# Idle products, tiles loaded singly, stores on another queue and sums loaded first in a fused S4 convolution and feed-forward kernel

## The chip, the cores and the metric

One Trainium2 chip, one core. The metric is device time in microseconds (us) of one execution. In the text P is 128, the number of partitions; PE is TensorE, DVE VectorE, ACT ScalarE, POOL GpSimd and SP SyncE. A DMA is issued from the queue of an engine (`nc.sync`, `nc.scalar`, `nc.gpsimd`), and the issuing instruction takes its turn among that engine's other instructions.

## What is computed

The input x has 2048 rows of 576. The result is x plus two branches of its layer norm, all in float32:

```python
xn  = (x - mean) / sqrt(var + 1e-5)                  # over the 576 columns
# S4: a kernel K of length 2048 per column, 128 complex states
A, B, C = A_re + 1j*A_im, B_re + 1j*B_im, C_re + 1j*C_im
dt  = exp(log_dt)
K   = einsum("dn,dnl,dn->dl", C, exp(dt*A*l), dt*B).real
y   = irfft(rfft(pad(xn.T)) * rfft(pad(K)))[:, :2048].T + xn * Dskip
h   = silu(xn @ w1)                                  # w1: 576 x 4608
out = x + y + h @ w2                                 # w2: 4608 x 576
```

## The kernel before

**The feed-forward part.** The rows stand in 16 tiles of 128 (`j` from 0 to 15), four tiles in a block of 512; tiles 0 to 7 are the first half, 8 to 15 the second. The 36 pieces of 128 hidden features are taken in chunks of four (`c`; `FT` is 4, `NCH` 9). For float32 accuracy each operand is split in a high and a low part (`h`, `l`): ScalarE copies the high part in the rounded type, VectorE subtracts it from the source, and three products replace one. `load_w1` fetches two pieces of w1 (tile `w1r`), `split_w1` makes `w1h` and `w1l` of it; `load_w2` and `split_w2` do the same for w2 (`w2r`, `w2`). `up` (L281) makes the hidden features of a block in `ph`, takes the SiLU and splits it in `gh` and `gl`; `down` (L301) multiplies them with w2 in `po`, for two halves of 288 columns, and VectorE adds `po` to `acc`, which holds x at first. After the last chunk of the first half, `down` stores `acc[j]` to `dr0` in DRAM and, for each odd j, loads two tiles of the second half in the buffers that came free (L326 to L328).

**Layer norm and transposes.** `phase0` (L200) takes a pair of tiles: `load_x` (L162) loads x in four quarters of 32 partitions, `norm` takes the statistics on VectorE, the power -0.5 on GpSimd, and makes `xn` on VectorE for even tiles and on ScalarE for odd ones. `normed` transposes `xn` on TensorE (`put_xt`, tile `pt`) and splits it in `xh`, `xl`, `x4`. For the blocks of the second half the transposed tile goes to one buffer `xt` and from there to `dxt` in DRAM; `next_xt` loads it again later. `xn` is stored to `dxn` for the convolution.

**The convolution** goes on beside that as a generator `side()` (L1022), in stages: `kgen` makes K with sines and exponentials, `spread` reads `xn` from `dxn` and makes the first transform (stores to `d1u` on GpSimd's queue, L158, from one buffer `u1`), `spectral` multiplies in the frequency domain and stores to `d2` (from tile `yo`), and `tail` (L947) adds the result. For the second half's tiles `conv` adds inside `down`, in the same bank as the products. For tiles 0 to 7 `last(j)` adds to `r0`, the sums of the first half loaded from `dr0`: `add_conv` makes 16 small products in `py` from `ys`, VectorE adds `py` to `r0`, and every second `last` stores two tiles of `r0` to the output on GpSimd's queue. There are two `r0` buffers of two tiles each and six `ys` buffers (`AHEAD`).

**The second half** of the feed-forward part runs in a form with fewer products (`wino_ffn`, L427): products in `pa`, `pb`, `pc` (L444, L450) with weights that VectorE first combines, and sums of them on VectorE, `f` (L519) among them.

**The order.** `weave(fg, 276, sd)` interleaves the two generators: each time `ffn()` has yielded, `side()` goes on as long as its own mark, a share of 276 steps, lies behind. `tail()` yields such marks for its steps: the loads from `tail_at[0]` on, `tail_at[1]` apart, and the `last(j)` from `tail_at[2]` on, `tail_at[3]` apart. Before it, `side()` and `ffn()` are advanced once or twice by hand:

```python
    sd = side()
    next(sd)
    fg = ffn()
    next(fg)
    next(sd)
    weave(fg, 276, sd)
```

What is issued in that order is placed by a scheduler, which simulates the engines and builds the order of each engine from it; `tc.high_priority()` lifts an instruction and `behind(ins)` keeps what follows behind another instruction. `pins` keeps the instructions that serve for that. One change in the program so shifts the built order of every engine in many places.

Of the kernel before, what the change touches and what calls it, by code (L numbers as in the profile page):

```python
# [10 lines left out]
F32 = mybir.dt.float32  # L11
# [30 lines left out]
def kernel(  # L42
# [30 lines left out]
    def quarters(v, engines):  # L73

        for q in range(4):
            yield slice(32 * q, 32 * q + 32), v[q // 2, q % 2], engines[q % len(engines)]
# [85 lines left out]
    def load_x(j, pool, tag, engines):  # L162

        t = pool.tile([P, 2, D], F32, tag=tag, name=f"{tag}{j}")
        for ps, v, eng in quarters(xv, engines):
            eng.dma_start(t[ps], v[:, j:j + 2])
        pairs[j] = t
        return t[:, 0, :], t[:, 1, :]

# [5 lines left out]
    def norm(p0, js, xs):  # L175

        n = len(js)
        st = p0.tile([P, 2, 2, 6], F32, tag="st", name="st")
        mv = p0.tile([P, 2, 2], F32, tag="mv", name="mv")
        for i in range(n):  # L180
            for h in range(2):
                nc.vector.bn_stats(out=st[:, i, h, :], in_=xs[i][:, h * HD:(h + 1) * HD])
            nc.vector.bn_aggr(out=mv[:, i, :], in_=st[:, i, :, :])
        sd = p0.tile([P, 2], F32, tag="sd", name="sd")
        mb = p0.tile([P, 2], F32, tag="mb", name="mb")
        nc.vector.tensor_scalar(sd[:, :n], mv[:, :n, 1], 1e-5, None, op0=ALU.add)
        pins["sd"] = nc.gpsimd.tensor_tensor(sd[:, :n], sd[:, :n], mhalf[:, :n], op=ALU.pow).ins
        xn = p0.tile([P, 2, D], F32, tag="xn", name="xn") if js[0] < 8 else pairs[js[0]]
        for i, j in enumerate(js):
            if j % 2 == 0:  # L190
                pins["xn"] = nc.vector.tensor_scalar(xn[:, i, :], xs[i], mv[:, i, 0:1], sd[:, i:i + 1],
                                                 op0=ALU.subtract, op1=ALU.mult).ins
            else:
                nc.vector.scalar_tensor_tensor(mb[:, i:i + 1], mv[:, i, 0:1], -1.0, sd[:, i:i + 1],
                                               op0=ALU.mult, op1=ALU.mult)
                nc.scalar.activation(xn[:, i, :], xs[i], AF.Identity,
                                     scale=sd[:, i:i + 1], bias=mb[:, i:i + 1])
        return xn

    def phase0(p0, js):  # L200
        j0 = js[0]
        if j0 < 8:
            xs = load_x(j0, accp, "acc", (nc.sync, nc.scalar) if j0 < 4 else (nc.sync,))
            acc.update(zip(js, xs))
        else:
            xs = load_x(j0, p0, "xj", (nc.sync,))
        if j0:
            normed(p0, js, xs)
        else:
            for j, xj in zip(js, xs):  # L210
                normed(p0, (j,), (xj,))

    def normed(p0, js, xs):
        xn = norm(p0, js, xs)
        for i, j in enumerate(js):
            b, jj = divmod(j, 4)
            if b < 2:
                if jj == 0:
                    xts[b] = new_xt(b)
                c = slice(jj * P, (jj + 1) * P)  # L220
                xh, xl, x4 = xts[b]
                put_xt(xh[:, :, c], xl[:, :, c], x4[:, c], xn[:, i, :])
            else:
                xt = p0.tile([P, 9, P], F32R, tag="xt", name="xt", bufs=1)
                put_xt(xt[:, 0:4, :], xt[:, 4:8, :], xt[:, 8, :], xn[:, i, :])
                nc.sync.dma_start(dxt[b - 2][:, :, jj * P:(jj + 1) * P], xt.bitcast(F32))
        nc.sync.dma_start(dxn[:, js[0]:js[0] + len(js)], xn[:, :len(js)])

    def ffn():
        w2v = w2.rearrange("(t p) d -> p t d", p=P)  # L230
# [31 lines left out]
        def load_w2(half, c, t):  # L262

            first = half == 0 and c == 0
            r2 = (pa if first else kfp).tile([P, D], F32, tag="w2r", name="w2r", bufs=4 if first else 2)
            pins["load"] = nc.sync.dma_start(r2, w2v[:, c * FT + t, :]).ins
            R2[half, c, t] = r2
# [33 lines left out]
        def down(blk, jj, terms=None):  # L301
            half, c, b = blk
            j = 8 * half + 4 * b + jj
            js = slice(jj * P, (jj + 1) * P)
            if half == 1 and c == NCH - 1 and jj % 2 == 0:
                for i, (pool, tag) in enumerate(((ps2, "ps2"), (ps1, "ps1"))):
                    begun[j + i] = [pool.tile([P, 512], F32, tag=tag, name="po") for _ in range(2)]
                conv((j, j + 1), (begun[j], begun[j + 1]))
                for i in range(2):
                    conv_load(j + i + AHEAD)  # L310
            terms = terms or [(G[blk, t], W2[half, c, t]) for t in range(FT)]
            for h in range(2):
                hs = slice(h * HD, (h + 1) * HD)
                po = begun[j][h] if j in begun else ps2.tile([P, 512], F32, tag="ps2", name="po")
                n = 0
                for gs, ws in terms:
                    for g, w in ((0, 0), (0, 1), (1, 0)):
                        pins["pe"] = nc.tensor.matmul(po[:, :HD], gs[g][:, js], ws[:, w, hs],  # L318
                                                      start=n == 0 and j not in begun, stop=n == 3 * len(terms) - 1,
                                                      skip_group_check=j in begun).ins  # L320
                        n += 1
                with tc.high_priority():
                    nc.vector.tensor_add(acc[j][:, hs], po[:, :HD], acc[j][:, hs])  # L323
            if half == 0 and c == NCH - 1:
                rows = slice(j * P, (j + 1) * P)
                nc.sync.dma_start(dr0[rows, :], acc[j])  # L326
                if j % 2:
                    acc[7 + j], acc[8 + j] = load_x(7 + j, accp, "acc", (nc.sync,))  # L328

        def next_xt(b):  # L330
            xt = new_xt(2 + b)
# [4 lines left out]

        for t in (0, 2):
            load_w1(0, 0, t)
        for t in (0, 2):
            split_w1(0, 0, t)  # L340
        for t in range(FT):
            load_w2(0, 0, t)
        for t in range(FT):
            split_w2(0, 0, t)
        yield 0
# [601 lines left out]
    def tail():  # L947

        r0s = {}

        def load_r0(j):
            r0s[j] = yp.tile([P, 2, D], F32, tag="r0", name="r0", bufs=2)
            nc.sync.dma_start(r0s[j], dr0[j * P:(j + 2) * P, :].rearrange("(i p) d -> p i d", p=P))

        def last(j):
            add_conv(j, r0s[j - j % 2][:, j % 2, :])
            conv_load(j + AHEAD)
            if j % 2:
                store(r0s[j - 1], j - 1, (nc.gpsimd,))

        steps, at = [], tail_at[0]
        for j in range(8):
            for f in (conv_load, load_r0)[j >= AHEAD:2 - j % 2]:
                steps.append((at, f, j))
                at += tail_at[1]
        steps += [(tail_at[2] + j * tail_at[3], last, j) for j in range(8)]
        for at, f, j in sorted(steps, key=lambda v: v[0]):
            yield at
            with behind(pins["load"]):
                f(j)  # L970
# [51 lines left out]
    def side():  # L1022
        nonlocal s4, kl, yp, pa, kfp, tail_at
        marks = (0.1357, 0.613, 0.855)
        tail_at = (0.893, 0.003, 0.930, 0.005)
        with tc.tile_pool(name="pa", bufs=4) as pa:
            for js in ((0, 1), (2, 3), (4, 5), (6, 7)):
                with behind(pins["xt3"] if js[0] > 2 else None):
                    phase0(pa, js)
                pins[f"xt{js[1]}"], pins[f"xt{js[1]}s"] = pins["xt_v"], pins["xt_s"]  # L1030
                if js[0] == 2:
                    yield 0
            yield 0
        with tc.tile_pool(name="kf", bufs=1) as kfp:
            for n in ("f", "rho", "phi"):
                kf[n] = kfp.tile([P, D], F32, name=n + "T")
            with tc.tile_pool(name="nat", bufs=1) as nat, tc.tile_pool(name="pb", bufs=2) as pb:
                nt = natural(nat)
                tiles = iter(range(8, NJ, 2))
                for at, tables in ((0.0, 1), (0.02, 0), (0.035, 0), (gate_of(1), 1), (0.06, 0), (gate_of(2), 1), (0.08, 0), (0.085, 1)):  # L1040
                    yield at
                    if tables:
                        next(nt, None)
                    else:
                        j = next(tiles)
                        with behind(pins["gl"]):
                            phase0(pb, (j, j + 1))
            with behind(pins["sd"]):
                nc.gpsimd.dma_start(f1, cf1)
            nc.sync.dma_start(vt, cv)  # L1050
# [19 lines left out]
        yp = ctx.enter_context(tc.tile_pool(name="yp", bufs=3))  # L1070
        yield from tail()

    sd = side()
    next(sd)
    fg = ffn()
    next(fg)
    next(sd)
    weave(fg, 276, sd)
    for j in range(8, 14, 2):
        store(pairs[j], j, (nc.sync, nc.gpsimd))  # L1080
# [80 lines left out]
```

## Time and profile before

| | us |
|---|---|
| median of 3 timed runs | 1136.39 |
| lowest, highest | 1133.1, 1138.12 |
| the profiled execution | 1141.59 |
| its span in the trace | 1139.8 |
| busy: TensorE | 1104.0 (97%) |
| busy: VectorE | 955.5 (84%) |
| busy: ScalarE | 721.1 (63%) |
| busy: GpSimd | 113.4 (10%) |
| DMA | 176.04 MB, mean 154 GB/s |

The trace is of one execution. Its views: busy time by engine; the waits (who waited for whom, total us, times, longest); the chain of work that ended last, followed back from the end; the timeline of instructions; windows (the share of each engine in a stretch, with the granted clock of TensorE, 1.00 being full speed); and the DMA issues, with the size and the median time from issue to landing. A matmul's end is modelled with its pipeline, so the durations of two products overlap and a busy TensorE is not one at its peak.

### The profile page before, as it was taken

The numbers are of one execution on the slowest core, as the hardware profiler recorded it, in microseconds if no ns is written. First come the engines' busy times: TensorE is split into PE (matmuls) and PEld (weight loads), VectorE is DVE, ScalarE is ACT, GpSimd is POOL, SyncE is SP. The second block draws the span as 40 slices with busy tenths as digits, with TensorE's granted clock in tenths as the row PEclk, the third lists the DMA queues.
The fourth block names the chain that finished last, engine by engine and source line by source line (L and its number), as shares of the span: only waits on it lengthen the run. The fifth ranks groups of instructions, "written<-read, shape, count | busy, mean of one in ns | idle before, by whom it ended". The sixth has DMA issues, their size and how long they took to land.

```text
span 1139.8 us, 23099 instructions
## 1 busy us (share of the span) xinstructions
PE 1104.0 (97%) x9101; PEld 991.5 (87%) x9101; DVE 955.5 (84%) x1631; ACT 721.1 (63%) x1269; POOL 113.4 (10%) x206
## 2 busy tenths in 40 slices
PE   6999999999999999999989999999999999999798
PEld 5998989888988899899988889999989899998576
DVE  6698898999999999999979988988888888884432
ACT  4665456676677666676747646887867777772210
POOL 1001000000000000000000002112112112210111
PEclk9999999999999999999989999999999999999899
DMA  9456523536263625376844137556455556547964
GB/s 274 131 160 197 165 97 101 144 109 167 83 166 108 188 86 150 109 218 215 230 124 115 54 64 219 153 172 181 141 161 148 171 171 187 176 121 180 260 172 109
DMA packets 171405, 176.04 MB, mean 154 GB/s; under 512 B 88432, under 2 KB 136576, under 8 KB 170656
## 3 DMA queue, kind: packets, MB, share of 16 engines
q1 hardware_dynamic: 150128, 120.91, 38.4%
q0 software_dynamic: 20784, 52.76, 14.7%
q8 instruction: 72, 1.18, 0.4%
q10 hardware_dynamic: 384, 0.89, 0.3%
q14 instruction: 37, 0.30, 0.1%
HBM read 112.00 MB, written 62.60 MB: 153 GB/s over the span
## 4 chain that ended last, share of the span: by engine, by line
PE 52%; DVE 21%; DMA 10%; issue 7%; ACT 7%; SPq 1%; POOL 1%; DVEq 0%; ACTq 0%; POOLq 0%
PE po L318 23%; PE ph L289 12%; DMA w1r<-in_B_w_dram 5%; PE pb L444 3%; DVE acc L323 2%; PE kp L855 2%; PE pc L444 2%; DMA w2r<-in_B_w_dram 1%; DVE th L798 1%; DMA ys<-d 1%; DVE S L834 1%; DVE C L834 1%; PE pb L986 1%; PE pu L986 1%; DVE gl L299 1%
## 5 line engine op out<-in xcount | busy, mean ns | idle before, releaser
L318 PE MATMUL po<-w,gh 128*128 128x288 f32 x2304 | 479.5, 297 | 8.2 <-ACT gh L298 3.8
L318 PEld LDWEIGHTS po<-w,gh 128*128 128x128 f32 x2304 | 378.2, 189 | 26.7 <-issue 5.6
L318 PE MATMUL po<-w,gl 128*128 128x288 f32 x1152 | 337.3, 297 | 0.4 <-DVE gl L299 0.4
L318 PEld LDWEIGHTS po<-w,gl 128*128 128x128 f32 x1152 | 216.2, 189 | 3.9 <-issue 1.4
L323 DVE TENSOR_TENSOR acc<-po,acc 128x288 f32<-128x288 f32 x296 | 130.5, 451 | 61.9 <-PE po L318 60.6
L289 PE MATMUL ph<-xh,w1h 128*128 128x512 f32 (+1 forms) x368 | 99.7, 389 | 0.9 <-ACT xh L124 0.6
L289 PE MATMUL ph<-xl,w1h 128*128 128x512 f32 (+1 forms) x368 | 99.3, 387 | 0.0
L289 PE MATMUL ph<-xh,w1l 128*128 128x512 f32 (+1 forms) x368 | 98.1, 383 | 0.0
L297 ACT ACTIVATE gf<-ph 128x512 f32<-128x512 f32 (+1 forms) x92 | 53.1, 577 | 48.8 <-PE ph L291 36.0
L289 PEld LDWEIGHTS ph<-xl,w1h 128*128 128x128 f32 x368 | 67.7, 192 | 12.9
L289 PEld LDWEIGHTS ph<-xh,w1l 128*128 128x128 f32 x368 | 66.8, 190 | 12.0
L289 PEld LDWEIGHTS ph<-xh,w1h 128*128 128x128 f32 x368 | 65.5, 192 | 11.3 <-ACT xh L124 0.9
L814 ACT ACTIVATE c<-th,magic 128x1040 f32<-128x1040 f32 x36 | 42.0, 1168 | 39.8 <-DVE C L835 31.6
L158 POOL DMA_DIRECT2D d1u<-u x32 | 17.3, 542 | 460.2 <-ACT u L157 460.2
L299 DVE TENSOR_TENSOR gl<-gf,gh 128x512 fp32r<-128x512 f32 (+1 forms) x92 | 60.6, 660 | 2.9 <-ACT gh L298 2.7
L298 ACT CAST gh<-gf 128x512 fp32r<-128x512 f32 (+1 forms) x92 | 55.2, 601 | 10.2 <-PE po L318 9.0
L816 ACT ACTIVATE c<-th 128x1040 f32<-128x1040 f32 x36 | 38.7, 1074 | 31.1 <-DVE th L815 31.1
L361 ACT CAST w1h<-w1r 128x512 fp32r<-128x512 f32 (+2 forms) x56 | 34.5, 619 | 37.1 <-DMA w1r<-in_B_w_dram 36.0
L892 POOL DMA_DIRECT2D m<-in_cm_dram x64 | 34.5, 539 | 223.7 <-PE pu L986 140.3
L362 DVE TENSOR_TENSOR w1l<-w1r,w1h 128x512 fp32r<-128x512 f32 (+2 forms) x56 | 38.3, 685 | 21.7 <-ACT w1h L361 21.7
L834 DVE TENSOR_TENSOR S<-th,C 128x1024 f32<-128x1024 f32 x36 | 43.9, 1219 | 9.8 <-ACT th L817 9.7
L461 DVE TENSOR_TENSOR gl<-gf,gh 128x512 fp32r<-128x512 f32 x56 | 37.8, 687 | 10.8 <-ACT gh L460 10.5
(268 smaller groups left out, 2372.2 us busy)
## 6 DMA issues: line engine op xcount, KB each, us to landing
w1r<-in_B_w_dram SPq DMA_DIRECT2D x35, 512.0 KB, 4.2
dw<-w SPq DMA_DIRECT2D x28, 576.0 KB, 4.7
w<-dw POOLq DMA_DIRECT2D x28, 576.0 KB, 5.8
w2r<-in_B_w_dram SPq DMA_DIRECT2D x44, 288.0 KB, 5.0
d1u<-u POOLq DMA_DIRECT2D x32, 288.0 KB, 2.7
d1k<-stage SPq DMA_DIRECT2D x18, 512.0 KB, 7.0
ur<-d1u SPq DMA_DIRECT2D x32, 288.0 KB, 4.0
kr<-d1k SPq DMA_DIRECT2D x32, 288.0 KB, 3.0
```

The source lines that it names most:

```text
L289: nc.tensor.matmul(ph, w[:, kt, :], v[:, kt, a:e], start=n + kt == 0, stop=False)
L297: nc.scalar.activation(gf, ph, AF.Silu)
L298: pins["gh"] = nc.scalar.copy(gh, gf).ins
L299: pins["gl"] = nc.vector.tensor_sub(gl, gf, gh).ins
L318: pins["pe"] = nc.tensor.matmul(po[:, :HD], gs[g][:, js], ws[:, w, hs], start=n == 0 and j not in begun, stop=n == 3 * len(terms) - 1, ski ...
L323: nc.vector.tensor_add(acc[j][:, hs], po[:, :HD], acc[j][:, hs])
L362: nc.vector.tensor_sub(l[:, :k], src, h[:, :k])
L444: pins["pe"] = nc.tensor.matmul(dst, a[:, kt], v[:, kt], start=start and n == 0, stop=stop and n == 5, skip_group_check=True).ins
L461: pins["gl"] = nc.vector.tensor_sub(gl, gf, gh).ins
L814: nc.scalar.activation(c65, th, AF.Identity, bias=magic)
L816: nc.scalar.activation(c65, th, AF.Abs)
L834: nc.vector.tensor_mul(ov3, t[:, :, 0:64].rearrange("n d (x y) -> n d x y", y=32), mv3)
```

## The change

At the outset, 14 products of a zeroed tile with itself go to TensorE ahead of all else (their result is used by nobody). Tiles 0 and 1 are loaded one by one, each in four quarters from SyncE's and ScalarE's queues, where the pair was one set of four loads; tiles 2 and 3 are loaded from SyncE's queue alone, and behind the loads of the first weights: `phase0` now yields between the load and the rest, `ffn()` between its loads and splits, and the driver advances the two in turn. The first weights of w2 are loaded ahead of the splits of w1. Where one tile is normalised alone (tiles 0 and 1), `xn` is made on VectorE for the odd tile too, and the work on tiles 2 and 3 is kept behind the last VectorE step of tile 1.

The stores to `dxt`, `dxn` and `dr0`, and the loads of the second half's tiles in `acc`, go to GpSimd's queue, where they were in SyncE's.

In the tail, each `r0` load comes ahead of the `ys` load that it was behind, and the first `last` is marked at 0.936 for 0.930.

```diff
--- before.py
+++ after.py
@@ -162,8 +162,12 @@
     def load_x(j, pool, tag, engines):
 
         t = pool.tile([P, 2, D], F32, tag=tag, name=f"{tag}{j}")
-        for ps, v, eng in quarters(xv, engines):
-            eng.dma_start(t[ps], v[:, j:j + 2])
+        for i in range(j, j + 2, 1 if j == 0 else 2):
+            for ps, v, eng in quarters(xv, engines):
+                if j == 0:
+                    eng.dma_start(t[ps, i], v[:, i])
+                else:
+                    eng.dma_start(t[ps], v[:, j:j + 2])
         pairs[j] = t
         return t[:, 0, :], t[:, 1, :]
 
@@ -187,7 +191,7 @@
         pins["sd"] = nc.gpsimd.tensor_tensor(sd[:, :n], sd[:, :n], mhalf[:, :n], op=ALU.pow).ins
         xn = p0.tile([P, 2, D], F32, tag="xn", name="xn") if js[0] < 8 else pairs[js[0]]
         for i, j in enumerate(js):
-            if j % 2 == 0:
+            if j % 2 == 0 or n == 1:
                 pins["xn"] = nc.vector.tensor_scalar(xn[:, i, :], xs[i], mv[:, i, 0:1], sd[:, i:i + 1],
                                                  op0=ALU.subtract, op1=ALU.mult).ins
             else:
@@ -200,12 +204,14 @@
     def phase0(p0, js):
         j0 = js[0]
         if j0 < 8:
-            xs = load_x(j0, accp, "acc", (nc.sync, nc.scalar) if j0 < 4 else (nc.sync,))
+            xs = load_x(j0, accp, "acc", (nc.sync, nc.scalar) if j0 == 0 else (nc.sync,))
             acc.update(zip(js, xs))
+            yield
         else:
             xs = load_x(j0, p0, "xj", (nc.sync,))
         if j0:
-            normed(p0, js, xs)
+            with behind(pins["xt1"] if j0 == 2 else None):
+                normed(p0, js, xs)
         else:
             for j, xj in zip(js, xs):
                 normed(p0, (j,), (xj,))
@@ -223,8 +229,8 @@
             else:
                 xt = p0.tile([P, 9, P], F32R, tag="xt", name="xt", bufs=1)
                 put_xt(xt[:, 0:4, :], xt[:, 4:8, :], xt[:, 8, :], xn[:, i, :])
-                nc.sync.dma_start(dxt[b - 2][:, :, jj * P:(jj + 1) * P], xt.bitcast(F32))
-        nc.sync.dma_start(dxn[:, js[0]:js[0] + len(js)], xn[:, :len(js)])
+                nc.gpsimd.dma_start(dxt[b - 2][:, :, jj * P:(jj + 1) * P], xt.bitcast(F32))
+        nc.gpsimd.dma_start(dxn[:, js[0]:js[0] + len(js)], xn[:, :len(js)])
 
     def ffn():
         w2v = w2.rearrange("(t p) d -> p t d", p=P)
@@ -323,9 +329,9 @@
                     nc.vector.tensor_add(acc[j][:, hs], po[:, :HD], acc[j][:, hs])
             if half == 0 and c == NCH - 1:
                 rows = slice(j * P, (j + 1) * P)
-                nc.sync.dma_start(dr0[rows, :], acc[j])
+                nc.gpsimd.dma_start(dr0[rows, :], acc[j])
                 if j % 2:
-                    acc[7 + j], acc[8 + j] = load_x(7 + j, accp, "acc", (nc.sync,))
+                    acc[7 + j], acc[8 + j] = load_x(7 + j, accp, "acc", (nc.gpsimd,))
 
         def next_xt(b):
             xt = new_xt(2 + b)
@@ -336,10 +342,12 @@
 
         for t in (0, 2):
             load_w1(0, 0, t)
+        yield 0
+        for t in range(FT):
+            load_w2(0, 0, t)
+        yield 0
         for t in (0, 2):
             split_w1(0, 0, t)
-        for t in range(FT):
-            load_w2(0, 0, t)
         for t in range(FT):
             split_w2(0, 0, t)
         yield 0
@@ -960,7 +968,7 @@
 
         steps, at = [], tail_at[0]
         for j in range(8):
-            for f in (conv_load, load_r0)[j >= AHEAD:2 - j % 2]:
+            for f in (load_r0, conv_load)[j % 2:2 - (j >= AHEAD)]:
                 steps.append((at, f, j))
                 at += tail_at[1]
         steps += [(tail_at[2] + j * tail_at[3], last, j) for j in range(8)]
@@ -1022,12 +1030,21 @@
     def side():
         nonlocal s4, kl, yp, pa, kfp, tail_at
         marks = (0.1357, 0.613, 0.855)
-        tail_at = (0.893, 0.003, 0.930, 0.005)
+        tail_at = (0.893, 0.003, 0.936, 0.005)
         with tc.tile_pool(name="pa", bufs=4) as pa:
+            zero = pa.tile([P, P], F32, name="zero", bufs=1)
+            nc.vector.memset(zero, 0.0)
+            idle = pss.tile([P, 512], F32, tag="pss", name="idle")
+            for _ in range(14):
+                nc.tensor.matmul(idle[:, :P], zero, zero, start=True, stop=True)
             for js in ((0, 1), (2, 3), (4, 5), (6, 7)):
                 with behind(pins["xt3"] if js[0] > 2 else None):
-                    phase0(pa, js)
+                    for _ in phase0(pa, js):
+                        if js[0] == 2:
+                            yield 0
                 pins[f"xt{js[1]}"], pins[f"xt{js[1]}s"] = pins["xt_v"], pins["xt_s"]
+                if js[0] == 0:
+                    yield 0
                 if js[0] == 2:
                     yield 0
             yield 0
@@ -1044,7 +1061,8 @@
                     else:
                         j = next(tiles)
                         with behind(pins["gl"]):
-                            phase0(pb, (j, j + 1))
+                            for _ in phase0(pb, (j, j + 1)):
+                                pass
             with behind(pins["sd"]):
                 nc.gpsimd.dma_start(f1, cf1)
             nc.sync.dma_start(vt, cv)
@@ -1070,11 +1088,9 @@
         yp = ctx.enter_context(tc.tile_pool(name="yp", bufs=3))
         yield from tail()
 
-    sd = side()
-    next(sd)
-    fg = ffn()
-    next(fg)
-    next(sd)
+    sd, fg = side(), ffn()
+    for g in (sd, fg, sd, fg, sd, fg, sd):
+        next(g)
     weave(fg, 276, sd)
     for j in range(8, 14, 2):
         store(pairs[j], j, (nc.sync, nc.gpsimd))
```

## The prediction

> **What bounds the kernel now.** I read the busy shares first, then what TensorE waited for, then the granted clock around the long waits, then the chain of waits at each of those places. The span, the busy shares, and TensorE's rows of the waits (total us, times, longest us):
>
> ```profile
> span 1139.8 us, 23099 instructions
> ```
> ```profile
> PE 1104.0 (97%) x9101; PEld 991.5 (87%) x9101; DVE 955.5 (84%) x1631; ACT 721.1 (63%) x1269; POOL 113.4 (10%) x206
> ```
> ```profile
> PE pt L123 <- DVE xn L191: 8.9, 1, 8.9
> PE pb L450 <- DVE f L519: 8.1, 1, 8.1
> PE po L318 <- ACT gh L298: 3.8, 2, 3.3
> ...
> PE po L318 <- ACT w L275: 1.7, 1, 1.7
> ```
>
> TensorE is busy for 1104.0 of 1139.8 us, and the change takes no product of the computation away. So a microsecond saved on another engine is worth nothing unless it shortens one of TensorE's few waits: 8.9 us at the outset, 8.1 us near the end, 3.3 us at 577 us and 1.7 us at 95 us. A wait costs more than itself, since the clock falls with it. The windows around the three later waits (length, each engine's busy time, granted clock, DMA share, GB/s):
>
> ```profile
> 94.00:102.00 8.00, 6.10 (x28) 4.93 (x27) 7.29 (x15) 6.05 (x9) 0.00 (x0) 0.79 0.85 247
> 576.00:586.00 10.00, 6.72 (x32) 6.49 (x32) 6.89 (x10) 5.50 (x12) 0.31 (x1) 0.66 0.54 171
> 1058.00:1071.00 13.00, 4.89 (x34) 3.71 (x34) 4.65 (x11) 1.14 (x2) 0.00 (x0) 0.74 1.09 255
> ```
>
> The clock was 0.79, 0.66 and 0.74, that is 1.7, 3.4 and 3.4 us of full clock missing. Part of that falls inside the waits, so I count 1.7, 2.0 and 2.5 us of slow products on top (the cuts in the last two are my choice). The places cost 3.4, 5.3 and 10.6 us.
>
> **The outset.** The chain of waits there, three rows of the timeline, and the sizes of what is loaded:
>
> ```profile
> 3.27 7.66 DMA w1r<-in_B_w_dram
> ...
> 11.03 1.35 ACT w1h L257 x2
> 12.38 0.49 ACT xh L124
> ```
> ```profile
> 8.91 1.12 PE L123 MATMUL pt<-ident,xn 128*128 128x128 f32 x4 [8.91 <-DVE xn L191]
> ```
> ```profile
> 12.92 2.07 PE L289 MATMUL ph<-xh,w1h 128*128 128x256 f32 x8 [0.57 <-ACT xh L124]
> ```
> ```profile
> 21.89 0.64 PE L289 MATMUL ph<-xh,w1h 128*128 128x256 f32 x4
> ```
> ```profile
> acc<-in_A_u_dram SPq DMA_DIRECT2D x28, 144.0 KB, 3.6
> ```
> ```profile
> w1r<-in_B_w_dram POOLq DMA_DIRECT2D x1, 512.0 KB, 8.5
> ```
>
> The first real product starts at 12.92, not when tile 0 is normalised: the first weights land at 10.93, ScalarE splits them until 12.38 and only then copies tile 1's xh. Loading tile 0 singly can bring the transposes forward by some 2 us, but in the built order ScalarE still has both w1h casts ahead of tile 1's copy, so the start remains the landing plus 2.0. Ahead of that landing stood four tiles, eight quarters of 144 KB, and the first weight piece, of which 512 KB are in the row: 1664 KB. In the changed order two tiles and two pieces stand there, 1600 KB, and the later pair of tiles behind them. So the first piece lands at about the same time or somewhat earlier, and the second, which stood behind four tiles, with it. I let the start move by 0 to 1 us.
>
> The fourteen idle products are over by then. A 128x128 product took at most 0.28 us (1.12 over 4), so they cover 4 us at most, and TensorE then has only ten transposes until the weights are in, a gap of 2 us or more. A 128x256 product takes 0.26 us at 12.92 (2.07 over 8) and at most 0.16 at 21.89, so the slow stretch costs some 40% of its time, 2.5 us if it lasts 6. The row of 94 to 102 shows the clock missing 1.7 us around a wait of 1.7, so I expect it low again for a part of the first products. The Trainium skill, "TensorE: Matmul & The Clock Gate", Part 1, says the clock is released after about 3.4 us of sustained products and falls back after an idle window of that length; the 1.7 us that a wait of 1.7 cost at 95 us is shorter than that, and by that rule the warm-up would last through a gap of 2 to 3 us. If it does, VectorE is next: four statistics of tiles 2 and 3 now stand between its w1l splits, and the transposes of those tiles stand in TensorE's order ahead of the second halves. I take a gain of 1.5 us; the ends are a loss of 1 (tiles 2 and 3, loaded later, hold TensorE) and a gain of 5 (start 1 earlier, 2.5 from the full clock, 1.5 of holds between the early products).
>
> **The stores on gpsimd's queue.** At 95 us the chain, ScalarE's row there, and the transit of 576 KB on either queue:
>
> ```profile
> 79.09 8.09 DMA dxt<-xt
> ...
> 91.78 4.15 DMA w2r<-in_B_w_dram
> ```
> ```profile
> 87.26 0.59 ACT L124 CAST xt<-pt 128x512 fp32r<-128x512 f32 x1 [6.10 <-DMA dxt<-xt]
> ```
> ```profile
> dw<-w SPq DMA_DIRECT2D x28, 576.0 KB, 4.7
> w<-dw POOLq DMA_DIRECT2D x28, 576.0 KB, 5.8
> ```
>
> There is one xt buffer, so ScalarE sat 6.1 us until the store of the tile before had landed, 8.09 us after its issue, because it went into SyncE's queue behind tile loads and most of a weight load. Its casts then came late, the w2r buffer was freed late, the next w2r was asked for at 91.78, and TensorE stood. On gpsimd's queue nothing is ahead of the store. The nearest rows for 576 KB are 4.7 us (SyncE) and 5.8 us (gpsimd); I take 5.8, by the queue, so what stands behind it moves 2.3 us earlier and the 1.7 us wait goes: a gain of 3.4, bounds 0 and 3.4. What is late next is still ScalarE at the following store, held 2 us less. On gpsimd the powers of tiles 12 and 13 are now queued behind three such stores, but in the built order VectorE writes those xt ahead of using the powers, so they cannot hold VectorE longer than its own order does.
>
> At 577 us the w2r load stood on SyncE behind stores of acc and loads into it. The chain, SyncE's waits, and gpsimd's largest:
>
> ```profile
> 573.41 4.97 DMA w2r<-in_B_w_dram
> ```
> ```profile
> SPq L166 <- DMA dr<-acc: 13.7, 4, 4.4
> ...
> SPq L326 <- DVE acc L323: 11.5, 4, 4.8
> ```
> ```profile
> POOL d1u L158 <- ACT u L157: 460.2, 32, 46.3
> ```
>
> SyncE's 13.7 and 11.5 us of waiting go to gpsimd, which stands idle 460 us ahead of its d1u stores. The w2r loads then wait only for their buffer. I take 4 of the 5.3 us, since a buffer may hold a part; bounds 0 and 5.3. The cover is that slack: two d1u stores now stand directly behind loads of acc that wait for a store to dr0; what it costs if the slack is not there is the last rival.
>
> The Trainium skill, "SBUF — State Buffer", section "SBUF: two separate sides", speaks against all of this: a DMA issued from GpSimd's queue needs descriptors, which GpSimd cannot write while VectorE holds the port that they share. VectorE is 84% busy, yet the two rows for 576 KB differ by 1.1 us, and no run here shows more of it.
>
> **The tail.** SyncE's longest wait, the chain, the rate, the transits, and two rows that price TensorE's products:
>
> ```profile
> SPq L993 <- DMA d<-yo: 15.6, 1, 15.6
> ```
> ```profile
> 1031.28 2.36 DMA d<-yo
> ```
> ```profile
> 1055.07 10.61 DMA w1r<-in_B_w_dram
> ```
> ```profile
> 1066.79 0.69 DVE f L519
> ```
> ```profile
> 1040.00:1060.00 20.00, 18.85 (x150) 15.16 (x148) 6.08 (x13) 2.41 (x5) 1.96 (x4) 1.00 1.11 247
> ```
> ```profile
> r<-dr SPq DMA_DIRECT2D x4, 576.0 KB, 8.0
> out_dram<-r POOLq DMA_DIRECT2D x16, 144.0 KB, 6.0
> ```
> ```profile
> 1099.14 3.19 PE po L318 x24
> 1102.33 1.38 PE pb L444 x6
> ```
>
> SyncE idles 15.6 us because the first ys load needs the last yo in DRAM. Then twelve ys loads, two r0 loads and the last w1r go out at once, the DMA engines are full (share 1.11 at 247 GB/s), and w1r lands at 1065.7 (1055.07 + 10.61), 34.4 us after the last yo store was issued. VectorE has the split of that w1r ahead of f, which ends at 1067.5, so TensorE wanted f at 1059.4, 28.1 us after that store. With r0 of tiles 0 and 1 first in the queue, its 576 KB move inside the 15.6 us; at 247 GB/s that frees 2.4 us. Counting both built orders by the last two rows (0.133 and 0.23 us per product), TensorE has 30.2 us of products from the last yo to that point after the change and 27.8 before: 2.4 us more. So the wait shrinks from 8.1 to 3.3 us and the slow clock behind it from 2.5 to about 1.3: a gain of 6.0. Bounds: 2.4 (only the load counts) and 10.6.
>
> The later start of the added convolutions (0.936 for 0.930) has a price. By the same count tile 0's py products stand 61.5 us of products before the end, not 72.2, and tile 4's follow tile 1's by only 9.6 us instead of 13.3. In between, r0 must be stored (6.0 us) and the next one loaded into its buffer (8.0 us), with some 2 us to add and issue: 16 us. VectorE would wait up to 6.4 us there; TensorE's three po buffers and the products that don't need r0 cover some 4 to 5 by my estimate. I book 0, bounds 0 and 4, the far end with the slow clock behind the remaining 2.
>
> **The sum.** 1.5 + 3.4 + 4.0 + 6.0 = 14.9 us. The profiled execution took 1141.59 (span 1139.8), so it would take 1126.7. The median of the three timed runs, 1136.39, is 5.2 below that execution; against it the forecast is 1136.4 − 14.9 = 1121.5.
>
> **The rivals.**
> *The stores land no sooner on gpsimd*, by the rule above, or because the DMA engines are as full for one queue as for the other: the waits at 95 and 577 stay, 1121.5 + 3.4 + 4.0 = 1129. For: 5.8 is above 4.7. Against: 8.09 was a place in a queue, not a rate. Chance 0.17.
> *The r0 wait takes the place of the w1r wait*: of the tail's 6, 2.4 stay and 4 are lost, 1121.5 + 7.6 = 1129. For: 16 against 9.6 + 5 us. Against: with the backlog cleared earlier, the store and the load meet emptier engines than those of their rows. Chance 0.14.
> *The change does not do what it says*: both of these, or the same waits at other places, since the order that the scheduler builds differs in nearly all stages; 1136. Chance 0.10.
> *Slower: loads of acc hold the d1u stores on gpsimd.* There is one u1 buffer. A d1u store held by 4.4 us (the longest wait for dr<-acc) and some 2 us of issues holds ScalarE's next u1 copy, and in its order gh, on which TensorE waits. Two stores stand so: 12.8 us, and 2 us of slow clock behind each. With the gain at 577 lost as well: 1121.5 + 4 + 16.8 = 1142. It decides if ScalarE copies the next u1 within 6.4 us of the last. Against: the 460 us of idle over 32 stores, 14 us each. Chance 0.13.
>
> **How the numbers follow.** The forecast has 0.46. Its own range is 1111 (start 5, tail 10.6, 577 whole: 9.4 less) to 1132 (start −1, 577 nothing, tail 4 less: 10.5 more). With the two rivals at 1129 and the one at 1136, I give 1111 to 1138; the slow case is left out. About 0.5% (5.7 us) is what a measurement of this kernel can tell from no change. Below 1130.7 fall nearly all of the forecast and some 0.20 of the two at 1129: 0.64. Within 0.5% lie the rest of these and over half of the case at 1136: 0.19. Slower: 0.17.
>
> **What would show it.** Right: an r0 load stands ahead of SyncE's wait for d<-yo; f's wait at L450 falls to about 3 us; no wait for w at 95 or for gh at 577, and the clock full there; the first product at 12 to 13 us. Wrong: a wait of VectorE for r<-dr with TensorE behind it; dxt landing in 8 us or more from gpsimd; ScalarE waiting for d1u near 550. The forecast is wrong as a whole if TensorE's idle time does not shrink by some 10 us.

## The result and the profile after

The changed kernel is slower: 1152.83 us median (1149.97 to 1154.7) against 1136.38 (1133.1 to 1138.12), a ratio of 1.0146 with a 95% interval of 1.0113 to 1.0179. The profiled execution took 1154.7 us, its span is 1152.5. The page after, span and busy shares:

```profile
span 1152.5 us, 23170 instructions
...
PE 1112.4 (97%) x9129; PEld 997.0 (87%) x9129; DVE 958.5 (83%) x1632; ACT 718.9 (62%) x1268; POOL 136.6 (12%) x247
```

TensorE is as busy as before, in shares, over a span that is 12.7 us longer; GpSimd's share rose by 2 points. Its waits (total us, times, longest us):

```profile
PE ph L295 <- ACT w1h L263: 7.1, 2, 6.2
PE po L324 <- DVE acc L329: 5.5, 6, 1.8
PE pb L458 <- DVE f L527: 4.3, 1, 4.3
PE pu L994 <- ACT kb L920: 3.0, 1, 3.0
PE po L324 <- ACT gh L468: 2.8, 1, 2.8
PE pt L123 <- DVE xn L195: 2.6, 2, 2.3
```

The four waits that the prediction went after are gone or shorter: 8.9 at the outset is 2.6 beside the idle products, 8.1 for f is 4.3, those for gh at 577 and for w at 95 have left the list. In their place stand others: 6.2 us for w1h, 3.0 for kb and 2.8 for gh, none of which the kernel before had at these places. The windows around them (length, busy time of each engine, granted clock, DMA share, GB/s):

```profile
560.00:580.00 20.00, 13.76 (x74) 12.23 (x72) 12.92 (x20) 9.26 (x12) 3.91 (x8) 0.83 0.64 183
700.00:712.00 12.00, 9.24 (x43) 7.85 (x42) 5.83 (x13) 8.73 (x19) 1.28 (x3) 0.83 0.81 273
908.00:916.00 8.00, 4.96 (x32) 4.36 (x31) 3.65 (x8) 3.38 (x8) 0.00 (x0) 1.00 0.41 143
```

Where the 12.7 us lie is seen when both traces are cut at equal work, not at equal times. The windows of the kernel before, from the point at which TensorE has done 140 us of products to 480, 600 and 940, and those of the changed kernel between the same points:

```profile
162.00:545.00 383.00, 381.59 (x4016) 344.02 (x4015) 366.78 (x540) 262.19 (x391) 16.78 (x31) 1.00 0.48 141
545.00:686.00 141.00, 136.12 (x1307) 122.34 (x1307) 123.20 (x182) 82.25 (x125) 6.90 (x13) 0.98 0.43 110
686.00:1037.00 351.00, 347.50 (x2173) 320.54 (x2172) 294.44 (x567) 266.13 (x571) 62.55 (x116) 1.00 0.55 164
```
```profile
163.00:552.00 389.00, 384.01 (x4029) 344.26 (x4028) 375.35 (x552) 264.02 (x394) 20.99 (x39) 1.00 0.48 140
552.00:693.00 141.00, 134.69 (x1290) 120.69 (x1289) 122.73 (x181) 83.16 (x125) 16.10 (x30) 0.98 0.43 111
693.00:1053.00 360.00, 351.40 (x2174) 322.66 (x2173) 295.10 (x566) 265.53 (x571) 60.94 (x114) 0.99 0.54 162
```

The middle stretches take 875 us before and 890 after: 15 us, of which the tail gives some 2.5 back. In the last of them, 9 us longer, the change edits nothing but the place of the first r0 load in its last 10 us: no step of it touches the convolution's spectral stage and the products of the second half's form (`wino_ffn`) that run there. What differs in it is only the order that the scheduler built. TensorE's listed waits there add up to 8.4 us, for 3.4 before, and the granted clock was low for longer, behind the two long waits of the changed kernel and behind the one (2.0 us, for kb) of the kernel before:

```profile
707.00:715.00 8.00, 6.28 (x17) 5.10 (x18) 6.94 (x13) 7.46 (x16) 0.00 (x0) 0.57 0.33 87
916.00:920.00 4.00, 4.00 (x12) 3.08 (x12) 3.85 (x10) 2.76 (x6) 0.53 (x1) 0.57 0.24 52
```
```profile
834.00:839.00 5.00, 4.44 (x18) 3.96 (x19) 4.26 (x11) 4.58 (x11) 0.54 (x1) 0.66 0.21 36
```

That is some 5 us of full clock missing for 1.7. Waits and clock together so account for nearly all of the 9 us. In the first of the stretches TensorE was idle for 5.0 us, for 1.4 before, with the clock full: behind several short waits (2.1 us for additions to acc, 1.4 for kt). The rest of what that stretch lost lies in intervals too short to be listed, and its cause stays open. The chain of the changed kernel at the two long waits of the last stretch, and gpsimd's timeline at the first:

```profile
699.42 6.86 DMA kr<-d1k
...
706.35 0.67 ACT kh L985
...
707.05 1.11 ACT gf L467 x2
708.16 0.52 ACT gh L468
```
```profile
698.62 2.12 POOL L479 DMA_DIRECT2D w<-dw  x4 [6.14 <-PE po L324]
```
```profile
906.67 6.43 DMA w1r<-in_B_w_dram
...
913.20 0.51 ACT w1h L369
...
914.87 0.40 ACT kb L920
```

In both, ScalarE's order puts a copy that needs a load (kh, w1h) ahead of the one on which TensorE waits (gh, kb), and the load takes 6 to 7 us, about twice its median of 3.1 (kr) or 3.6 to 3.7 (the pieces of w1r); at the first place four loads of w were issued within the same 2 us. The kernel before has such loads too (one of kr, issued at 696 us, took 6.7 us to land), but TensorE has no wait at these places.

The theory from this: **the order**. The edits move the scheduler's simulated times, it builds another order for nearly all stages, and this order has more and longer waits; the edits' own costs are small. The rivals: **the queue** (the stores and loads on gpsimd's queue cost, above all at 560 us) and **the outset** (the idle products and the reordered loads cost).

### The profile page after: what moved, and what is told of

Its sections match the earlier page's. It is cut to its first block, busy times and chain, and to the rows that moved or that the text cites. A ratio compares the mean times of both kernels' runs of the same rounds, so it can differ in the third digit from the quotient of the medians.

```text
span 1152.5 us, 23170 instructions
## 1 busy us (share of the span) xinstructions
PE 1112.4 (97%) x9129; PEld 997.0 (87%) x9129; DVE 958.5 (83%) x1632; ACT 718.9 (62%) x1268; POOL 136.6 (12%) x247
## 4 chain that ended last, share of the span: by engine, by line
PE 61%; DVE 19%; DMA 8%; ACT 6%; issue 3%; SPq 1%; POOL 0%; DVEq 0%; ACTq 0%; POOLq 0%
PE po L324 28%; PE ph L295 12%; PE pb L452 4%; DMA w1r<-in_B_w_dram 3%; PE pc L452 2%; PE kp L863 2%; PE pb L994 2%; PE pu L994 1%; PE pk L994 1%; DVE acc L329 1%; DMA acc<-in_A_u_dram 1%; PE z L878 1%; DVE th L806 1%; DVE gl L305 1%; DVE th L823 1%
## 5 line engine op out<-in xcount | busy, mean ns | idle before, releaser
L324 PEld LDWEIGHTS po<-w,gh 128*128 128x128 f32 x2304 | 378.3, 189 | 29.8 <-DVE acc L329 9.2
L370 DVE TENSOR_TENSOR w1l<-w1r,w1h 128x512 fp32r<-128x512 f32 (+2 forms) x56 | 38.3, 684 | 19.1 <-ACT w1h L369 18.9
L842 DVE TENSOR_TENSOR S<-th,C 128x1024 f32<-128x1024 f32 x36 | 43.8, 1218 | 9.0 <-ACT th L825 9.0
L469 DVE TENSOR_TENSOR gl<-gf,gh 128x512 fp32r<-128x512 f32 x56 | 38.0, 686 | 10.7 <-ACT gh L468 10.4
```

What stands on the lines that cost most here:

```text
L370: nc.vector.tensor_sub(l[:, :k], src, h[:, :k])
L842: nc.vector.tensor_mul(ov3, t[:, :, 0:64].rearrange("n d (x y) -> n d x y", y=32), mv3)
```

## The experiments

Every ratio is to the kernel before, run beside it. First, each part by itself, where the built order could be held.

**Ten idle products.** The kernel before with

```diff
+            idle = pss.tile([P, 512], F32, tag="pss", name="idle")
+            for _ in range(10):
+                nc.tensor.matmul(idle[:, :P], zero, zero, start=True, stop=True)
```

> The kernel before with ten idle products at the outset and nothing else; the built order of every engine stays that of the kernel before beyond the first 40 us. Theory of the order (the loss of 16 us lies in the order that the scheduler builds, which differs in nearly all stages): as before, within 3 us, waits at 95, 577, 832 and 1059 us at their old places. Theory of the outset (the products themselves, with the clock that they set, cost time): slower by several us.

1138.62 us, ratio 1.0011 (0.9994 to 1.0028): no change that can be measured. The products themselves neither cost nor gain anything clear.

**Fourteen**, `range(14)`.

> The kernel before with fourteen idle products and nothing else. Four products more, some 1 us, shift the scheduler's simulated times so that the built order becomes another one from the first stages on; from about 600 us it is that of the changed kernel up to the tail. Theory of the order: 5 to 12 us slower than the ten products, with waits near 706 and 912 us as in the changed kernel and none at 832. Theory of the queue (the loss comes from the stores and loads on gpsimd's queue) and theory of the outset: within 1 us of the ten products.

1139.98, ratio 1.0028 (1.0009 to 1.0048). Waits of 1.6 and 1.9 us appear where the changed kernel has 2.8 and 3.0, so the order brings the waits; but it is only 1.4 us slower than the ten, not 5 to 12, since this kernel's stretch ahead of 680 us is better than that of before. An order is not good or bad as a whole.

**The tail alone:**

```diff
-            for f in (conv_load, load_r0)[j >= AHEAD:2 - j % 2]:
+            for f in (load_r0, conv_load)[j % 2:2 - (j >= AHEAD)]:
-        tail_at = (0.893, 0.003, 0.930, 0.005)
+        tail_at = (0.893, 0.003, 0.936, 0.005)
```

> The kernel before with the two edits of the tail alone (r0 loads first, 0.936 for 0.930); the built order differs only in the last 100 us. By the changed kernel's trace the tail gained 3 to 4 us: 1131 to 1134. Forecast of the prediction: 6 us, 1130. Rival of the prediction (the r0 wait takes its place): 1137 to 1140.

1135.04, ratio 0.9985 (0.9968 to 1.0001): 1.9 us less, with an interval that just reaches no change. TensorE's longest wait in the tail, and VectorE's for r0:

```profile
PE py L1005 <- DVE r L1016: 6.8, 1, 6.8
```
```profile
DVE r L1016 <- DMA r<-dr: 5.0, 1, 5.0
```

The wait for f (8.1) has gone, and the wait for r0 stands in its place, as the second rival had it.

**The dr0 stores and acc loads alone:**

```diff
-                nc.sync.dma_start(dr0[rows, :], acc[j])
+                nc.gpsimd.dma_start(dr0[rows, :], acc[j])
-                    acc[7 + j], acc[8 + j] = load_x(7 + j, accp, "acc", (nc.sync,))
+                    acc[7 + j], acc[8 + j] = load_x(7 + j, accp, "acc", (nc.gpsimd,))
```

> The kernel before with the dr0 stores and the loads of acc on gpsimd's queue and nothing else; the built order differs only between about 500 and 680 us. Theory of the queue: slower by 4 us or more, with a wait for w1h or for acc near 560 as in the changed kernel. Theory of the order, and the prediction: the wait of 3.4 us at 577 goes, 1132 to 1136; waits of other lengths may come in the reordered stretch.

1134.09, ratio 0.9969 (0.9955 to 0.9984): faster. The window around the old wait at 577 us, first this kernel, then the kernel before:

```profile
560.00:590.00 30.00, 30.00 (x303) 27.01 (x303) 29.24 (x42) 21.13 (x31) 5.78 (x12) 1.00 0.45 144
```
```profile
560.00:590.00 30.00, 26.72 (x270) 24.11 (x269) 24.88 (x36) 15.89 (x25) 1.09 (x2) 0.89 0.58 175
```

TensorE runs through at full clock. This move does what was forecast, and no cost of the queue shows for these stores and loads.

Then whole parts, whose built order is another one.

**The outset alone** (the changed kernel with stores and tail as before).

> The outset alone: idle products, tiles 0 and 1 singly, first weights ahead of tiles 2 and 3; stores and tail as before. Its built order is that of the fourteen idle products alone (1140) from about 40 us on. Theory of the outset (the rest of the outset loses): 1145 or more, with the loss ahead of 45 us. Theory of the order: 1137 to 1141, like the fourteen idle products.

1145.31, ratio 1.0071 (1.0046 to 1.0095). A time that fits the theory of the outset, but not its place: its trace has lost 16.5 us in the first 40 us of products against 16.3 before, and the rest later (table below). But it is 5 us slower than the fourteen products alone, whose order it shares from 40 us on, and 1.9 us of that do lie in the first 40 (16.5 for 14.6); where the rest comes from is not shown.

**All stores alone.**

> The stores to dxt, dxn and dr0 and the loads of acc on gpsimd's queue, nothing else. The dr0 stores and acc loads alone gave 1134.1, with the order of before outside 500 to 680 us; those to dxt and dxn make the built order another one from 60 us on. Theory of the queue and its order: 1145 to 1150, with a wait for w1h near 560 us and others near 100, 705 and 912, since this is where the changed kernel lost most. Theory of the outset: 1133 to 1137.

1144.99, ratio 1.0061 (1.0037 to 1.0085). Slower, but the wait for w1h near 560 is only 1.4 us; the loss is in the stretches that follow the other order.

**The changed kernel without the stores.**

> The changed kernel with all stores and the acc loads back in SyncE's queue. Theory of the queue: the 16 us go nearly all, 1136 to 1140. Theory of the outset: they stay, 1148 or more.

1144.19, ratio 1.0051 (1.003 to 1.0073). By the ratio a third of the loss stays, so neither rival holds alone.

**The changed kernel without the tail's edits.**

> The changed kernel with the tail of before; the built order differs from it in the last 100 us only. The tail's two edits alone gave 1.9 us on the kernel before. If they give as much here: 1154 to 1157. If the changed kernel's tail loses instead (the r0 wait, 4.7 us in its trace): 1150 or less.

1156.98, ratio 1.0166 (1.0134 to 1.0199): as expected from the 1.9 us; the intervals overlap that of the changed kernel.

These parts leave the loss spread: 8 and 8 us for outset and stores against 16 for all. The cross that separates edits from order is a number that none of them touches, the mark at which `side()` begins with K. At 0.135 instead of 0.1357 the scheduler builds before's late order for the changed kernel, and the changed kernel's late order for the kernel before.

**The changed kernel, all edits, mark 0.135:**

```diff
-        marks = (0.1357, 0.613, 0.855)
+        marks = (0.135, 0.613, 0.855)
```

> The changed kernel, all its edits kept, with one more: the mark of the stage that makes K is 0.135 for 0.1357. The scheduler then builds, from about 680 us to the tail, the order of the kernel before, and in 500 to 680 us nearly that of the run that moved only the dr0 stores and acc loads. Theory of the order (the loss is in the order built, not in what the edits do by themselves): 1133 to 1141, without the waits at 560, 706 and 912 us. Theory that the edits themselves cost (queue, outset): 1148 or more, as without the mark.

1140.39, ratio 1.0034 (1.0015 to 1.0053). Three quarters of the loss have gone with all edits in place. The load of kr near 695 us is as slow as ever in this trace (7.4 us to land), and TensorE does not wait behind it: the long load alone does not make the wait. Its last windows, to be held against 141 and 360 above:

```profile
549.00:685.00 136.00, 133.50 (x1307) 120.02 (x1306) 124.01 (x183) 82.50 (x125) 15.42 (x29) 1.00 0.44 115
685.00:1036.00 351.00, 347.27 (x2179) 320.17 (x2178) 294.45 (x567) 265.68 (x572) 62.24 (x118) 1.00 0.56 165
```

**The kernel before, no edit, mark 0.135**, the same diff.

> The kernel before, none of the change's edits, with the mark 0.135 for 0.1357; the scheduler then builds from about 620 us on the order of the changed kernel up to the tail. Theory of the order: slower than before, 1140 to 1148, with waits near 706 and 912 us. Theory that the edits cost: 1136 to 1138.

1154.84, ratio 1.0161 (1.0139 to 1.0183): as much as the whole loss, without one of the edits, and 7 us beyond what was expected. That even the time is the same is chance: only the order from 600 to 940 is that of the changed kernel, and the 7.8 us more than before that it lost up to 480 (table below) lie in an order of its own. Its chain at the two places:

```profile
694.80 6.36 DMA kr<-d1k
...
701.24 0.67 ACT kh L977
...
701.94 1.11 ACT gf L459 x2
```
```profile
902.84 5.57 DMA w1r<-in_B_w_dram
...
908.51 0.51 ACT w1h L361
...
910.17 0.40 ACT kb L912
```

The same load, the same copy ahead of the same needed one, as in the changed kernel.

**The changed kernel with the dxt and dxn stores back on SyncE's queue.**

> The changed kernel with the stores to dxt and dxn back on SyncE's queue; the dr0 stores and acc loads stay on gpsimd's. The built order is that of the changed kernel from about 560 us on, and another one before. Theory of the order: the wait of 6 us at 560 goes, those at 706 and 912 stay, 1142 to 1148. Theory of the queue with the dr0 stores and acc loads as its cause: 1150 or more, the wait at 560 stays.

1149.88, ratio 1.0111 (1.0084 to 1.0138). A miss of the theory of the order in one point: a wait for w1h of 5.5 us stays. (The trace is of the fastest of its six executions, 1143.16 us.) It is in the order from there on, which this kernel shares with the changed one. That the dr0 stores and acc loads do not cause it by their queue is shown by their run alone and by the mark of 0.135, which have them on that queue and no such wait.

**The changed kernel without idle products**, the order otherwise the same.

> The changed kernel without the fourteen idle products; the built order of what is left is the same to the last instruction. If the idle products gain by the clock as the traces of the outset say (full clock at the first transposes, low again for some 3.4 us): 0 to 3 us slower than the changed kernel, 1153 to 1156. If they only delay: 1149 to 1152.

1159.58, ratio 1.0212 (1.0186 to 1.0239), some 7 us slower than the changed kernel, more than either theory gave. In its trace only 1.4 us of this are lost at the outset; 4.8 are in 160 to 550 us and 5.3 in the tail, where TensorE waits 6.3 us for f, for 4.3, and the granted clock was 0.92 over the last 105 us, for 0.96 over the last 100, some 4 us of full clock more. So even one and the same order loses a different time when its start is moved a little (the first product at 12.30 us for 12.02). Why is open.

The last three were for what stayed open.

**The mark by itself**: the kernel before with 0.1365, under which the order stays but for a short stretch.

> The kernel before with the mark 0.1365 for 0.1357: a change of the mark, on the side away from 0.135, under which the built order stays as it was but for a stretch of some 80 us near 450. Theory of the order: within 3 us of before, 1134 to 1140. If the mark itself, by the work that it moves, sets the time: well off, as 0.135 gave 1155.

1135.42, ratio 0.9994 (0.9978 to 1.0009). A mark moved about as far the other way, which leaves the late order as it was, changes nothing; so what 0.135 costs comes with the order.

**The parts that leave the order as it was, together**: ten idle products, dr0 stores and acc loads on gpsimd's queue, the tail's two edits.

> The kernel before with ten idle products, the dr0 stores and acc loads on gpsimd's queue, and the tail's two edits: those parts of the change that alone left the built order as it was outside the stretch that they touch (500 to 680 us and the tail). Theory of the order: the parts add, 1137 less 2.9 less 1.9 and 0 to 1.7 more, 1131 to 1134, faster than both kernels. If the parts cost once they are together, as theory of the edits has it: 1137 or more.

1131.31, ratio 0.9953 (0.9937 to 0.997): faster than both kernels, and the sum of the parts (1136.0 less 2.9, less 1.9, is 1131.2, with the idle products at nothing).

**The same with the r0 loads first, but 0.930.**

> The same with the r0 loads first but the added convolutions begun at 0.930 as before. If the wait of 6.8 us for r0 that the tail's edits brought comes from the later start (less time between a store of r0 and the next load): 2 to 5 us faster than with 0.936, 1128 to 1131. If the start at 0.936 is what shortens the wait for f: slower than that, 1133 to 1137.

1136.28, ratio 1.0007 (0.9992 to 1.0023), 5 us slower than with 0.936. VectorE's wait for r0 and TensorE's behind it:

```profile
DVE r L1016 <- DMA r<-dr: 11.4, 2, 9.5
```
```profile
PE po L318 <- DVE acc L323: 8.7, 4, 7.2
```

The later start does not bring the r0 wait, it shortens it (5.7 us in the run above). The loads put first bring it: in the kernel before, VectorE waited 0.6 us for r0 in the tail.

The time that each trace lost, by stretches of equal work. For each trace the products are summed at the interval between starts that the quickest quarter of their shape shows over all traces (1009.7 us, idle products at nothing); the table gives what the trace took beyond that, in us, up to the end of the last product, and the median that was timed. "Late order" is that of the stretch from 600 to 940.

| kernel | to 40 | to 140 | to 480 | to 600 | to 940 | end | late order | median |
|---|---|---|---|---|---|---|---|---|
| before | 16.3 | 5.9 | 42.5 | 21.5 | 11.2 | 27.6 | before's | 1136.38 |
| mark 0.1365 | 15.8 | 3.4 | 43.8 | 22.2 | 10.1 | 28.6 | before's | 1135.42 |
| tail | 16.0 | 4.2 | 42.5 | 17.1 | 10.5 | 25.8 | before's | 1135.04 |
| dr0, acc | 15.1 | 4.5 | 42.4 | 15.9 | 9.7 | 30.6 | before's | 1134.09 |
| ten idle | 15.6 | 3.3 | 42.4 | 20.5 | 10.3 | 29.8 | before's | 1138.62 |
| kept parts | 15.9 | 3.5 | 42.6 | 15.9 | 9.3 | 28.3 | before's | 1131.31 |
| changed, 0.135 | 16.3 | 5.4 | 47.0 | 16.6 | 10.4 | 30.9 | before's | 1140.39 |
| fourteen idle | 14.6 | 4.7 | 43.4 | 17.1 | 14.3 | 29.0 | changed | 1139.98 |
| outset | 16.5 | 5.7 | 43.9 | 16.9 | 15.5 | 28.0 | changed | 1145.31 |
| all stores | 17.6 | 3.5 | 47.0 | 14.4 | 18.0 | 30.2 | changed | 1144.99 |
| changed | 15.4 | 7.6 | 49.2 | 21.1 | 20.0 | 25.1 | changed | 1152.83 |
| before, 0.135 | 15.5 | 3.9 | 50.3 | 19.3 | 18.9 | 31.6 | changed | 1154.84 |

Column "to 940" is 9 to 11 under the one order and 14 to 20 under the other, with or without the edits. The five runs that the table leaves out fit: 15.7 to 18.2 for the four under the changed order (without the stores, without the tail's edits, dxt and dxn back, without idle products), 7.9 for the kept parts at 0.930. But under the one order the column still moves by 6 us, so the order brings the loss and does not alone set its size. Column "to 480" is 42 to 44 for before's order and for that of the fourteen products and the outset, and 47 to 50 for four others.

What is left open is the last quarter. The changed kernel with 0.135 is 9 us slower than the kept parts, and half of that is lost up to 480 (47.0 for 42.6), in an order of its own; whether the dxt and dxn stores, the outset or that order costs it was not separated.

## Why the prediction was wrong

The step that failed is the sum: it took four waits out of an otherwise unchanged trace. That the built order differs in nearly all stages was known and stood in the third rival, where it had a chance of 0.10 and the price of nothing, 1136; the fourth rival, the only one on the slow side, had another mechanism. An order that is built anew has waits of its own, and they came to some 20 us here (columns "to 480" and "to 940": 6.7 and 8.8 more than before, and 6.2 us at 560). Nothing bounded them in the sum or in the range. (The range has a slip besides: 1121.5 less 9.4 is 1112, not 1111.)

*The outset.* Forecast 1.5, lost time 16.3 against 15.4: 0.9. That is no gain shown: the other traces with all edits of the outset lost 15.2 to 16.5 there, and those with none of them 15.1 to 17.6. The first products start at 12.02 for 12.92, inside the 0 to 1 that was given. Timeline after:

```profile
1.15 5.12 PE L1039 MATMUL idle<-zero 128*128 128x128 f32 x28 [1.15 <-DVE zero L1036]
6.52 0.66 PE L123 MATMUL pt<-ident,xn 128*128 128x128 f32 x4 [0.25 <-DVE xn L195]
...
9.59 0.63 PE L123 MATMUL pt<-ident,xn 128*128 128x128 f32 x4 [2.31 <-DVE xn L195]
...
12.02 2.08 PE L295 MATMUL ph<-xh,w1h 128*128 128x256 f32 x8 [1.69 <-ACT xh L124]
```

The fourteen products are 28 records and take 5.1 us, not 4 at most. They do bring the full clock (four transposes in 0.66 for 1.12), and it is low again for the first products (2.08 over 8), as was expected from a gap that only ten transposes fill. The other case, in which the warm-up lasts through such a gap, did not come, though TensorE was idle for no more than 2.31 us in one piece.

*95 us.* The place was right and the mechanism half: the median of dxt's stores is 4.5 us on gpsimd, 4.4 before.

```profile
dxt<-xt POOLq DMA_DIRECT2D x8, 576.0 KB, 4.5
```

ScalarE's wait for them fell from 14.5 to 10.0 us. But the stretch to 140 lost 1.7 us more, since VectorE's order now puts statistics and table steps ahead of an addition to acc, for which TensorE waits 1.8 us. The same wait is also an example of a smaller error: the kernel before lost 5.9 there in its profiled execution, and the six other traces of the table that have its order there lost 3.3 to 4.5. In those TensorE waited 0.9 to 1.6 us for w too, but the granted clock stayed full (1.00 from 97 to 101 us with the mark 0.1365); the 1.7 us booked for slow products belonged to that one execution. It took 5.2 us more than the median, and the savings were subtracted from the median as if it had the same waits.

*577 us.* Right: the dr0 stores and acc loads alone take the wait away and gain 2.9 (2 to 5 by the interval) for 4.0. In the changed kernel the order puts the wait of 6.2 us for w1h at 560 in its place. Its chain:

```profile
561.24 0.17 SPq L250
...
562.68 3.42 DMA w1r<-in_B_w_dram
...
566.20 0.73 ACT w1h L263
```

*The tail.* Forecast 6.0, measured 1.9, by the interval 0 to 4. In the run of the tail alone the f wait went, the r0 wait came with 6.8: the second rival, to which 0.14 was given and which the prediction priced at a loss of 1.6. Its term "I book 0" is the one mis-sized: the cover of 4 to 5 us for the r0 wait was not there. Nor is the later start what brings that wait, as the prediction had it: with 0.930 VectorE waited 11.4 us for r0. In the changed kernel's own tail, which has another order, the f wait fell to 4.3 (3.3 was forecast), and VectorE's wait of 4.6 us for r0 did not reach TensorE.

*The stores on gpsimd's queue.* The medians from issue to landing hardly moved in the changed kernel: dr0's stores went from 5.0 to 4.2 us, the second half's loads of acc from 3.2 to 3.3, the dxt stores from 4.4 to 4.5; the three dxn stores of 576 KB from `xn` went from 3.4 to 4.3. The rule of the Trainium skill by which VectorE can starve such DMAs while it holds the port that it shares with GpSimd ("SBUF — State Buffer", "SBUF: two separate sides") does not show in these medians, at a VectorE that is 83% busy. In the run of all stores alone the acc loads took 4.8 and the dxt stores 5.1, in yet another order; what of that is the queue was not separated. ScalarE never waited for a d1u store, so the slower rival was wrong in its mechanism too.

## What to carry to other kernels

Where a scheduler builds the order from simulated times, an edit's effect has two parts: what it does in its place, and what the order built anew does everywhere else; here some 20 us lost against some 5 gained. So compare the built orders first, give the reshuffle a price and a range of its own (here all nine kernels whose late order was another one came out slower, by 3 to 23 us in 1137, the effect of their edits included), and measure an edit under an order that is held, for instance by moving a neutral constant until the rest of the order comes out as before. To find where two traces part, cut them at equal work, not at equal times.

## What was not expected of the hardware

One order, run without the idle products and so with its start moved a little, lost some 7 us more, most of it far from the outset (the changed kernel with and without its idle products). And an issue on SyncE's queue can itself take long: the first load of w1r behind two stores of stage tiles took 5.95 us to issue, against 0.39 for its kind at 905 us; the wait at 560 begins there. The waits put 5.8 us of it down to a VectorE step that this load neither reads nor writes (`al`, L801), so what holds the issue is open. It is not peculiar to this order: the load at the same place, one of w2r, took 4.25 us to issue in the kernel before and 5.86 with the dr0 stores and acc loads alone, where TensorE has no wait from 560 to 600. The long issue alone does not make the wait. The changed kernel, then the run of the dr0 stores and acc loads:

```profile
551.60 3.76 SPq L891 DMA_DIRECT2D d1k<-stage  x2
555.46 5.95 SPq L250 DMA_DIRECT2D w1r<-in_B_w_dram  x1
```
```profile
550.12 5.86 SPq L266 DMA_DIRECT2D w2r<-in_B_w_dram  x1
```
